# A Fourier mixing layer and a gated feed-forward layer in one kernel: where GpSimd's fold operations and the odd tables stand in the order of work

## The chip, the cores and the metric

The kernel runs on one core of a Trainium2 chip, in fp32. Its time is the device time of one execution in microseconds; smaller is better. The profile is of one execution, taken by the hardware profiler. The engines are called as in the profile: PE is TensorE's matmul and PEld its weight load, DVE is VectorE, ACT is ScalarE, POOL is GpSimd, SP issues most DMAs.

## The reference

Two layers follow one another.

- Mixing: X = FFT along the sequence, then FFT along the features, of x with shape (8, 3008, 256); only the real part is kept.
- Feed-forward, on the 8 x 3008 = 24064 rows of that result: gate = sigmoid(x @ w_gate), val = x @ w_val, out = (gate * val) @ w_out, with w_gate and w_val of 256 x 1536 and w_out of 1536 x 256.

```python
X = np.fft.fft(x, axis=1)
X = np.fft.fft(X, axis=2)
x = X.real.astype(np.float32).reshape(B * S, D)
gate = 1.0 / (1.0 + np.exp(-(x @ w_gate)))
val = x @ w_val
return (gate * val @ w_out).astype(np.float32)
```

## The kernel before

The real part of the two-dimensional transform needs only cosine and sine sums over the sequence, of folded data. For each batch the rows s, S-s, M+s and M-s (M = 1504) lie in four slots of one SBUF tile `x4`, 128 partitions x 4 slots x 6 rows x 256 features. **Folding** (`fold_ops`, L371) replaces the slots by their sums and differences, over the sequence and over the features. For batches 1 to 7 it is 24 operations, all on GpSimd, in this order: three `point` (L378) and a `first` (L382) for slots 0 and 1; the same four for slots 2 and 3 (operations 0 to 7); six `across` (L391; 8 to 13); three `feat` (a memset, L386, L388) on one pair of slots (14 to 16); four sums over halves of the rows (L407; 17 to 20); three `feat` on the other pair (21 to 23). After `feat` 14 to 16, six `turn` operations on VectorE (L418) rotate the odd half with the tangents in `ST[3]` and `ST[4]`.

The **sequence transform** of a batch (`whole`, `half`) is a run of matmuls of the folded tile with cosine and sine tables, in four groups of 24; it writes `ev` and `od`, which ScalarE and VectorE turn into `pk` and `qk` (`then`, `places`). The first two groups, of odd k, read `ST[1]` and the pair folded by operations 14 to 16; the last two, of even k, read the pair folded by operations 21 to 23. 

The **tables** come in two shapes. Batch 0 uses the one loaded at the start. At step 42 `table_again` loads another shape by four DMAs into the same place. `table_odd` then makes `ST[1]`, the table for odd k, out of neighbouring columns: two sums (L211), two halvings (L213, on ScalarE), and six small copies and memsets of the end columns (L214 to L220); and the tangents, three small operations on VectorE (L221 to L223).

The **main loop** (L843) has 576 steps: 8 batches x 6 chunks of up to 252 columns x 12 blocks of 128 of the 1536 hidden features, so 72 steps a batch. Step i does this, in program order: TensorE multiplies `G1`, the weights joined with the feature transform, by `pk` (`front_a`); ScalarE takes the sigmoid of step i-1 (`gate_a`), copies step i (`part`, L598) and puts the seeds of step i+1 into PSUM (`seed`, L582); VectorE and ScalarE finish the products of step i-1 (`gate_b`); TensorE multiplies by the output weights (`back`) and `G2` by `qk` (`front_b`). Three steps make a group, whose 9 products h are extended by 13 sums on GpSimd (L640, `H_SUMS`): seven when its second step is finished, six, some of them in the place of earlier ones, when its third is. `back`, for a group five steps earlier, reads only h in its part 0; blocks 13, 11 and 12 of sf in part 1; and five more blocks of sf in part 2. VectorE adds up the output of a finished chunk, two or three operations a step (`later`, L687), and transposes it.

What stands beside the main loop is put into a dictionary `side` by `at(i, f)`, and is emitted at the end of step i, after `front_b` and the `later` operations. Every engine runs its own instructions in the order in which they are emitted. So a fold operation stands in GpSimd's queue behind the sums of the steps before, and before those of the steps after it, and GpSimd reaches it some two steps later than TensorE passes the step that emits it.

Around the change: `folds(slots)` spreads 24 operations evenly over a list of steps `slots`. The sequence transform of batch b+1 is emitted at step `g0`: 64 for batch 1, and 72 b + 40 for the others, so 112 for batch 2 and 184 for batch 3. Before the change a slot is any step with i % 12 < 4, up to `g0`: 24 to 27, 36 to 39, 48 to 51 and 60 to 63 for batch 1; 72 to 75, 84 to 87, 96 to 99 and 108 to 111 for batch 2; and six such clusters for each later batch. Four successive slots get 6 operations for batches 1 and 2, and 4 for the others. `e_sums` at step 40 makes the rows `ed` with feature 128 of all later batches; `table_odd` stands at step 46.

Of the kernel before, what the change touches and what calls it, by code (L numbers as in the profile page):

```python
# [11 lines left out]
ALU = mybir.AluOpType  # L12
# [42 lines left out]
HP = 64  # L55
# [26 lines left out]
def kernel(  # L82
# [10 lines left out]
    nc = tc.nc  # L93
# [7 lines left out]
    NO = (M // 2) // 2  # L101
# [9 lines left out]
    NJ = NO // 2 + 1  # L111
# [17 lines left out]
    op = ctx.enter_context(tc.tile_pool(name="op", bufs=1))  # L129
# [3 lines left out]
    def mm(o, l, r, start, stop):  # L133
        nc.tensor.matmul(o, l, r, start=start, stop=stop, skip_group_check=True)  # L134

    def bank(name, other=None):
        if other is not None:
            return pso.tile([P, 512], F32, name=name, tag=f"po{other}")
        return psx.tile([P, 512], F32, name=name, tag="x")
# [4 lines left out]
    def load_x(b):  # L144
        X[b] = xp.tile([P, 4, NQ, D], F32, name="x4", tag="x4")
        for h in range(0, 4, 2):
            if b:
                nc.sync.dma_start(out=X[b][:, h : h + 2], in_=XR[b][:, h : h + 2])
            else:
                nc.sync.dma_start(out=X[b][0:NP, h : h + 2], in_=xf[b, :, h : h + 2])  # L150
# [3 lines left out]
    def mirror_x(b):  # L154


        copy = nc.sync.dma_start
        src = xf[b]
        dst = XR[b] = dram.tile([P, 4, NQ, D], F32, name=f"xr{b}")
        ops = [lambda: copy(out=dst[HP - 2 : HP, :, NQ - 1],  # L160
                            in_=zero[:, :, 0:D].to_broadcast([2, 4, D]))]

        def rows(par):
            copy(out=dst[par * HP : (par + 1) * HP, :, 0:N3], in_=src[0:HP, :, par:NQ:2])

        def mirror(par, q):
            t = M // 2 - 2 * q - par
            lo, p0, n = par * HP, t // NQ, HP - 2 * ((par, q) == (0, N3 - 1))
            copy(out=dst[lo : lo + n, :, N3 + q].rearrange("p h d -> h p d"),
                 in_=src[p0 - n + 1 : p0 + 1, :, t % NQ].rearrange("p h d -> h p d")[:, ::-1])  # L170
        for par in range(2):
            ops.append(lambda par=par: rows(par))
            ops += [lambda par=par, q=q: mirror(par, q) for q in range(N3)]
        return ops
# [3 lines left out]
    ST = [const.tile([P, 2, NQ, NE + NO], F32, name="st", tag="st")]  # L178
# [28 lines left out]
    def table_odd():  # L207

        odd, j4 = ST[0][:, :, :, NE:], ST[1]
        for t in range(2):  # L210
            nc.gpsimd.tensor_tensor(j4[:, t, :, 1 : NJ - 1], odd[:, t, :, 2::2], odd[:, t, :, 1 : NO - 1 : 2],  # L211
                                    op=ALU.add)
            nc.scalar.mul(j4[:, t, :, 1 : NJ - 1], j4[:, t, :, 1 : NJ - 1], 0.5)  # L213
        nc.gpsimd.tensor_copy(j4[:, 0, :, 0:1], odd[:, 0, :, 0:1])  # L214
        nc.gpsimd.memset(j4[:, 1, :, 0:1], 0.0)

        for par in range(2):
            rows = slice(par * HP, (par + 1) * HP)
            nc.gpsimd.tensor_copy(j4[rows, par, :, NJ - 1 :], odd[rows, par, :, NO - 1 :])
            nc.gpsimd.memset(j4[rows, 1 - par, :, NJ - 1 :], 0.0)  # L220
        nc.vector.reciprocal(ST[4], odd[:, 0, :, 0])  # L221
        nc.vector.tensor_tensor(ST[3], odd[:, 1, :, 0], ST[4], op=ALU.mult)
        nc.vector.tensor_scalar(out=ST[4], in0=ST[3], scalar1=-1.0, scalar2=None, op0=ALU.mult)  # L223

# [227 lines left out]
    def half(b, w, d, blk, sn, other=None):  # L454


        c0, n = ((0, NE), (NE, 2 * NJ if b else NO))[blk]
        ev, od = [bank(name, other and other[i])[:, 0:n] for i, name in enumerate(("ev", "od"))]

        def sums(*qs):  # L460
            for q in sorted(qs, key=lambda q: q % 2):
                mm((ev, od)[q % 2], w(q), ST[0][0:NP, int(sn), q, c0 : c0 + n], q < 2, q >= NQ - 2)

        def both():

            for r in range(2):
                for q in range(N3):
                    for par, sum_ in enumerate((ev, od)):
                        rows = slice(par * HP, par * HP + HP - 1 - (par and q == N3 - 1))
                        if blk:  # L470
                            out_, wq = sum_[:, r * NJ : (r + 1) * NJ], q + N3 * r
                            tab = ST[1][rows, r ^ int(sn), q]
                        else:
                            out_, wq = sum_[:, r::2], q + N3 * (r ^ int(sn))
                            tab = ST[0][rows, int(sn), q, r:NE:2]
                        mm(out_, w(wq)[rows], tab, q == 0 and r == 0, q == N3 - 1)

        def then():
            a = evp.tile([P, 2 * NJ], F32, name="a", tag="a")
            if b and blk:  # L480
                for par, sum_ in enumerate((ev, od)):
                    f = a[:, par * NJ : (par + 1) * NJ]
                    nc.scalar.copy(f, sum_[:, 0:NJ])
                    for r, op_ in enumerate((ALU.add, ALU.subtract)):
                        nc.vector.tensor_tensor(ST[2][:, par, r::2], f[:, r : NJ - 1 + r],  # L485
                                                sum_[:, NJ + r : 2 * NJ - 1 + r], op=op_)
                return lambda: places(d, blk, sn, ST[2][:, 0], ST[2][:, 1])
            a = a[:, 0:n]
            nc.scalar.copy(a, ev)
            return lambda: places(d, blk, sn, a, od)  # L490
        return sums, then, both

    def places(d, blk, sn, ev, od):
        nc.vector.tensor_tensor(d[:, blk : blk + 2 * ev.shape[1] - 1 : 2], ev, od, op=ALU.add)
        lo, hi = (od, ev) if sn else (ev, od)
        top = M - blk
        nc.vector.tensor_tensor(d[:, top : top - 2 * NO + 1 : -2], lo[:, 0:NO], hi[:, 0:NO],  # L497
                                op=ALU.subtract)

    def whole(b, blk, what):  # L500
        _, then, both = seq_group(b, blk, what, (2, 3) if what else (0, 1))
        both()
        return then()

    def seq_start(b):
        PQE[b] = [pqp.tile([P, NK + 1], F32, name=name, tag=name) for name in ("pk", "qk")]
        if not b:
            PQE[b].append(op.tile([P, NK + 1], F32, name="ek", tag="os"))
        for t in PQE[b]:
            nc.vector.memset(t[:, NK:], 0.0)  # L510
# [279 lines left out]
    def at(i, *fs):  # L790
        side.setdefault(i, []).extend(fs)
# [14 lines left out]
    i0 = NFT  # L806
# [7 lines left out]
    at(3 * i0, e_fold)  # L814
    at(3 * i0 + 4, lambda: e_sums()())
    at(3 * i0 + 6, table_again)
    at(3 * i0 + 10, table_odd)
    for i in range(i0, count, i0):
        at(i - 8, lambda i=i: e_rows(i))

    for b in range(B - 1):
        s0 = b * per
        g0 = s0 + 3 * i0 + 4 if b else 5 * i0 + 4


        slots = [i for i in range(s0 - 2 * i0 if b > 1 else s0 if b else 2 * i0, g0) if i % i0 < 4]

        def folds(slots, b=b):
            ops = fold_ops(b + 1, 2)
            for i, f in enumerate(ops):  # L830
                at(slots[i * len(slots) // len(ops)], f)
            for i, f in enumerate(TURN.pop(b + 1)):
                at(slots[-4 + i * 4 // 6], f)
        at(slots[0] - 1, lambda slots=slots, folds=folds: folds(slots))
        at(g0 - 2, lambda b=b: seq_start(b + 1))
        for blk in (1, 0):
            at(g0, *[lambda b=b, blk=blk, what=what: whole(b + 1, blk, what)() for what in range(2)])
        if b < B - 2:
            at(g0 + 1, lambda b=b: load_x(b + 2))
            for i, f in zip(calm(s0 if b else 3 * i0), mirror_x(b + 2)):  # L840
                at(i, f)
# [80 lines left out]
```

## Time and profile before

| | us |
|---|---|
| median of 3 runs | 1974.49 |
| lowest and highest run | 1964.23, 1974.6 |
| the profiled execution | 1966.45 |
| its span, first to last instruction | 1964.6 |
| PE busy | 1920.6 |
| POOL busy | 1639.9 |
| DVE busy | 1567.0 |
| ACT busy | 1341.0 |

A row of a group of instructions gives the line, the engine, the operation, what it writes and reads, the shape, how often it runs, its busy time in all, the mean ns of one, and the idle time of the engine before it with what ended it. A row in order of time gives start, length, engine, line, operation and tiles, and in brackets the engine's idle time before it and what ended that. A row of a stretch gives its ends and length, then the busy time of each engine with its number of instructions, the granted TensorE clock as a share of full speed, and the DMA share and rate. All matmuls have line L134, that of a helper; they are told apart by their tiles: `pf<-pk,G` is `front_a`, `pf<-qk,G` is `front_b`, `po` is `back`, `ev` and `od` are the sequence transform.

### The profile page before, as it was taken

How to read it: one execution, taken by the hardware profiler on the slowest of the kernel's cores; microseconds unless marked ns; L12 is line 12 of the kernel's file. 1: busy time of each engine (PE TensorE's matmuls, PEld its weight loads, DVE VectorE, ACT ScalarE, POOL GpSimd, SP SyncE). 2: the span in 40 equal slices, each digit the busy share in tenths (PEclk: the TensorE clock that was granted, in tenths of full speed). 3: DMA queues.
4: the chain of work that ended last, by engine and by line, in shares of the span. 5: the costliest groups of instructions: out<-in, count | busy, mean ns of one | idle time of the engine just before them, and what ended most of it. 6: DMA issues, size and time to landing. Idle time of an engine off the chain costs nothing.

```text
span 1964.6 us, 34539 instructions
## 1 busy us (share of the span) xinstructions
PE 1920.6 (98%) x11252; PEld 1791.5 (91%) x11252; DVE 1567.0 (80%) x3271; ACT 1341.0 (68%) x3124; POOL 1639.9 (83%) x2851
## 2 busy tenths in 40 slices
PE   6999899999999999999999999999999999999997
PEld 4889789998999999999999999999999999999997
DVE  7888797887788877888778887788878887777777
ACT  3567657665777767776777767777677776777775
POOL 3779898997889978897889878998788896777776
PEclk8999999999999999999999999999999999999999
DMA  8361413112012120222113121211210110011011
GB/s 269 89 133 27 102 39 110 46 24 78 18 46 52 21 78 14 54 51 64 29 22 77 21 78 22 44 53 20 81 20 14 19 23 14 14 21 21 14 19 27
DMA packets 169746, 96.78 MB, mean 49 GB/s; under 512 B 133858, under 2 KB 161636, under 8 KB 167020
## 3 DMA queue, kind: packets, MB, share of 16 engines
q1 hardware_dynamic: 167596, 94.02, 20.0%
q8 instruction: 90, 1.47, 0.3%
q10 hardware_dynamic: 1940, 0.56, 0.2%
q14 instruction: 88, 0.72, 0.1%
q0 software_dynamic: 32, 0.00, 0.0%
HBM read 69.83 MB, written 46.71 MB: 59 GB/s over the span
## 4 chain that ended last, share of the span: by engine, by line
PE 90%; DVE 5%; POOL 3%; ACT 1%; DMA 1%; issue 0%; SPq 0%; DVEq 0%; ACTq 0%; POOLq 0%
PE pf L134 47%; PE po L134 39%; PE ev L134 2%; POOL sf L640 2%; DVE c L687 1%; PE od L134 1%; DMA x<-in_xf_dram 1%; DVE h L636 1%; PE ps L134 1%; DVE z L622 1%; ACT z L635 0%; DVE st L485 0%; POOL x L407 0%; DVE pk L497 0%; POOL x L388 0%
## 5 line engine op out<-in xcount | busy, mean ns | idle before, releaser
L640 POOL TENSOR_TENSOR sf<-h 128x168 f32<-128x168 f32 (+1 forms) x960 | 552.3, 593 | 199.8 <-DVE h L636 199.7
L640 POOL TENSOR_TENSOR sf<-h,sf 128x168 f32<-128x168 f32 (+1 forms) x1152 | 661.5, 593 | 60.1 <-DVE h L636 60.1
L134 PE MATMUL pf<-qk,G 128*128 128x252 f32 (+1 forms) x2304 | 583.2, 376 | 7.8 <-ACT ae L598 5.6
L134 PE MATMUL pf<-pk,G 128*128 128x252 f32 (+1 forms) x2304 | 584.3, 376 | 0.0
L636 DVE TENSOR_TENSOR h<-z 128x252 f32<-128x252 f32 (+1 forms) x576 | 300.3, 521 | 332.1 <-ACT z L635 331.7
L582 ACT ACTIVATE pf<-ek,ge 128x252 f32<-128x252 f32 (+1 forms) x1128 | 531.5, 471 | 18.5
L134 PE MATMUL po<-sf,wf 128*128 128x168 f32 (+1 forms) x3072 | 530.8, 306 | 0.0
L598 ACT ACTIVATE ae<-pf 128x504 f32<-128x504 f32 (+1 forms) x569 | 335.0, 589 | 238.9 <-PE pf L134 238.4
L687 DVE TENSOR_TENSOR c<-c 128x168 f32<-128x168 f32 (+1 forms) x949 | 485.4, 542 | 5.5 <-ACT c L664 0.3
L134 PEld LDWEIGHTS pf<-pk,G 128*128 128x128 f32 x2304 | 437.0, 190 | 53.2 <-issue 2.3
L134 PEld LDWEIGHTS po<-sf,wf 128*128 128x128 f32 x3072 | 473.6, 190 | 8.3
L134 PE MATMUL po<-h,wf 128*128 128x168 f32 (+1 forms) x2688 | 477.1, 306 | 0.1
L134 PEld LDWEIGHTS po<-h,wf 128*128 128x128 f32 x2688 | 428.9, 191 | 17.1 <-DVE wf L357 0.3
L134 PEld LDWEIGHTS pf<-qk,G 128*128 128x128 f32 x2304 | 409.9, 190 | 35.3 <-ACT ae L598 7.4
L622 DVE TENSOR_TENSOR z<-ae,pf 128x504 f32<-128x504 f32 (+1 forms) x569 | 377.6, 664 | 21.3 <-ACT h L617 20.7
L617 ACT ACTIVATE h<-pf 128x252 f32<-128x252 f32 (+1 forms) x576 | 217.9, 378 | 161.2 <-PE pf L134 151.5
L635 ACT ACTIVATE z<-z 128x252 f32<-128x252 f32 (+1 forms) x576 | 231.6, 402 | 95.5 <-DVE z L622 74.2
L634 DVE TENSOR_TENSOR h<-h,pf 128x252 f32<-128x252 f32 (+1 forms) x576 | 231.9, 403 | 0.0
L640 POOL TENSOR_TENSOR sf<-sf 128x168 f32<-128x168 f32 (+1 forms) x192 | 111.6, 581 | 15.0
L640 POOL TENSOR_TENSOR sf<-sf,h 128x168 f32<-128x168 f32 (+1 forms) x192 | 107.4, 559 | 0.0
L134 PE MATMUL ev<-st,x 63*128 63x189 f32 (+3 forms) x372 | 77.1, 355 | 14.1 <-DVE x L388 7.5
L134 PEld LDWEIGHTS ev<-st,x 63*128 63x128 f32 (+1 forms) x372 | 63.5, 193 | 24.5 <-DVE x L388 7.9
(138 smaller groups left out, 905.4 us busy)
## 6 DMA issues: line engine op xcount, KB each, us to landing
x<-xr SPq DMA_DIRECT2D x14, 1536.0 KB
out_dram<-os SPq DMA_DIRECT2D x380, 56.0 KB
xr<-in_xf_dram SPq DMA_DIRECT2D x14, 768.0 KB
xr<-in_xf_dram SPq DMA_DIRECT2D x35, 256.0 KB
ek<-ed SPq DMA_DIRECT2D x39, 126.0 KB
out_dram<-os SPq DMA_DIRECT2D x288, 7.0 KB
st<-in_stab_dram SPq DMA_DIRECT2D x4, 1111.9 KB
x<-in_xf_dram SPq DMA_DIRECT2D x2, 1512.0 KB
```

The source lines that it names most:

```text
L134: nc.tensor.matmul(o, l, r, start=start, stop=stop, skip_group_check=True)
L582: nc.scalar.activation(PF[i][:, g], EK[i // NFT], AF.Copy, scale=ge[:, g, f : f + 1])
L598: nc.scalar.activation(AP[i], PF[i], AF.Copy, scale=2.0)
L617: nc.scalar.activation(H[p][:, fh, 0:n], PF[i][:, 0], AF.Sigmoid)
L622: nc.vector.tensor_tensor(z[:, :, ::-1], AP.pop(i), PF[i], op=ALU.subtract)
L634: nc.vector.tensor_tensor(h[:, fh, 0:n], h[:, fh, 0:n], PF.pop(i)[:, 1], op=ALU.mult)
L635: nc.scalar.activation(z[:, 0], z[:, 0], AF.Sigmoid)
L636: nc.vector.tensor_tensor(h[:, fh, n:], z[:, 0], z[:, 1], op=ALU.mult)
L640: nc.gpsimd.tensor_tensor(block(p, dst), block(p, a), block(p, b), op=(ALU.subtract, ALU.add)[op])
L687: engine.tensor_tensor(t[:, dst * R : (dst + 1) * R], *v, op=(ALU.subtract, ALU.add)[op])
```

## The change

`table_odd` no longer emits its work at once. It returns six functions, which are put at six successive steps, 54 to 59 (`at(4 * i0 + 6 + i, f)`; i0 is 12): the sum for the cosines, its halving, the sum for the sines, its halving, the ends, the tangents. The halvings are `tensor_scalar` on GpSimd in place of `mul` on ScalarE. The tangents stay on VectorE.

The slots of the folds end two steps sooner for every batch (`g0 - 2`), and for batches 1 and 2 a slot is any step with i % 12 < 6. So batch 1 has the slots 24 to 29, 36 to 41, 48 to 53, 60 and 61; batch 2 has 72 to 77, 84 to 89, 96 to 101, 108 and 109; 20 in place of 16, with 24 operations as before. Later batches have 22 in place of 24. The turns stay in the steps where they were: the last slot less one is now what the fourth slot from the end was.

```diff
     def table_odd():
         odd, j4 = ST[0][:, :, :, NE:], ST[1]
-        for t in range(2):
-            nc.gpsimd.tensor_tensor(j4[:, t, :, 1 : NJ - 1], odd[:, t, :, 2::2], odd[:, t, :, 1 : NO - 1 : 2],
-                                    op=ALU.add)
-            nc.scalar.mul(j4[:, t, :, 1 : NJ - 1], j4[:, t, :, 1 : NJ - 1], 0.5)
-        nc.gpsimd.tensor_copy(j4[:, 0, :, 0:1], odd[:, 0, :, 0:1])
...
-        nc.vector.reciprocal(ST[4], odd[:, 0, :, 0])
...
+        pool = nc.gpsimd
+
+        def inner(t):
+            pool.tensor_tensor(j4[:, t, :, 1 : NJ - 1], odd[:, t, :, 2::2], odd[:, t, :, 1 : NO - 1 : 2],
+                               op=ALU.add)
+
+        def half(t):
+            pool.tensor_scalar(out=j4[:, t, :, 1 : NJ - 1], in0=j4[:, t, :, 1 : NJ - 1], scalar1=0.5,
+                               scalar2=None, op0=ALU.mult)
+
+        def ends():
+            pool.tensor_copy(j4[:, 0, :, 0:1], odd[:, 0, :, 0:1])
+            pool.memset(j4[:, 1, :, 0:1], 0.0)
...
+        def tangent():
+            nc.vector.reciprocal(ST[4], odd[:, 0, :, 0])
...
+        return [lambda: inner(0), lambda: half(0), lambda: inner(1), lambda: half(1), ends, tangent]
...
-    at(3 * i0 + 10, table_odd)
+    at(4 * i0 + 5, lambda: [at(4 * i0 + 6 + i, f) for i, f in enumerate(table_odd())])
...
-        slots = [i for i in range(s0 - 2 * i0 if b > 1 else s0 if b else 2 * i0, g0) if i % i0 < 4]
+        slots = [i for i in range(s0 - 2 * i0 if b > 1 else s0 if b else 2 * i0, g0 - 2)
+                 if i % i0 < (4 if b > 1 else 6)]
...
             for i, f in enumerate(TURN.pop(b + 1)):
-                at(slots[-4 + i * 4 // 6], f)
+                at(slots[-1] - 1 + i * 4 // 6, f)
```

More of the change, by code (lines that the diff above doesn't have):

```diff
@@ L209, in table_odd @@
         odd, j4 = ST[0][:, :, :, NE:], ST[1]
-        for t in range(2):
-            nc.gpsimd.tensor_tensor(j4[:, t, :, 1 : NJ - 1], odd[:, t, :, 2::2], odd[:, t, :, 1 : NO - 1 : 2],
-                                    op=ALU.add)
-            nc.scalar.mul(j4[:, t, :, 1 : NJ - 1], j4[:, t, :, 1 : NJ - 1], 0.5)
-        nc.gpsimd.tensor_copy(j4[:, 0, :, 0:1], odd[:, 0, :, 0:1])
[L215 to L220, printed above, removed]
-        nc.vector.reciprocal(ST[4], odd[:, 0, :, 0])
-        nc.vector.tensor_tensor(ST[3], odd[:, 1, :, 0], ST[4], op=ALU.mult)
-        nc.vector.tensor_scalar(out=ST[4], in0=ST[3], scalar1=-1.0, scalar2=None, op0=ALU.mult)
+        pool = nc.gpsimd
[8 more added lines that the diff above has]
+            pool.memset(j4[:, 1, :, 0:1], 0.0)
+            for par in range(2):
+                rows = slice(par * HP, (par + 1) * HP)
+                pool.tensor_copy(j4[rows, par, :, NJ - 1 :], odd[rows, par, :, NO - 1 :])
+                pool.memset(j4[rows, 1 - par, :, NJ - 1 :], 0.0)
+        def tangent():
+            nc.vector.reciprocal(ST[4], odd[:, 0, :, 0])
+            nc.vector.tensor_tensor(ST[3], odd[:, 1, :, 0], ST[4], op=ALU.mult)
+            nc.vector.tensor_scalar(out=ST[4], in0=ST[3], scalar1=-1.0, scalar2=None, op0=ALU.mult)
+        return [lambda: inner(0), lambda: half(0), lambda: inner(1), lambda: half(1), ends, tangent]
     assert NPR == 6
```

## The prediction

> **What bounds the kernel now.** I read the page's busy shares, the chain of waits, the busy times by stretch, and each engine's instructions in order of time around every stretch where TensorE stood still. From the page:
>
> ```profile
> PE 1920.6 (98%) x11252; PEld 1791.5 (91%) x11252; DVE 1567.0 (80%) x3271; ACT 1341.0 (68%) x3124; POOL 1639.9 (83%) x2851
> ```
>
> TensorE is busy 98%, and beyond the first 125 us nearly all its idle time lies in a few places. A step is the time between the starts of two successive G x pk groups in TensorE's timeline: 3.12 us for chunks of 252 columns. Stretches cut at such starts (columns: time, length, busy us of PE, PEld, DVE, ACT, POOL, granted clock, DMA):
>
> ```profile
> 222.97:228.53 5.56, 3.40 (x20) 2.85 (x18) 4.26 (x8) 3.07 (x7) 4.62 (x12) 1.00 0.00 1
> 228.53:233.35 4.82, 4.82 (x19) 4.53 (x19) 3.14 (x9) 2.34 (x6) 3.63 (x7) 0.65 0.26 40
> 280.25:294.80 14.55, 11.88 (x116) 10.67 (x115) 12.49 (x26) 4.88 (x13) 12.58 (x23) 1.00 0.06 11
> 435.12:438.71 3.59, 3.39 (x19) 2.85 (x18) 3.44 (x8) 2.00 (x5) 3.51 (x6) 1.00 0.03 5
> 438.71:442.52 3.81, 3.42 (x20) 2.88 (x19) 3.66 (x8) 2.48 (x6) 3.81 (x6) 1.00 0.44 70
> 442.52:458.70 16.18, 13.51 (x115) 12.26 (x114) 12.55 (x26) 4.91 (x13) 12.64 (x23) 0.89 0.03 9
> 679.80:692.19 12.39, 12.12 (x115) 10.85 (x113) 11.00 (x23) 4.75 (x14) 9.51 (x18) 1.00 0.07 12
> ```
>
> These are steps 47, 48, 64, 110, 111, 112 and 184. Steps 64, 112 and 184 hold the sequence transform of batches 1, 2 and 3; 184 shows it undisturbed. In the chain of waits (total, times, longest) and in time order:
>
> ```profile
> ACT st L213 <- POOL st L211: 2.7, 2, 2.2
> PE ev L134 <- POOL x L388: 5.2, 2, 2.6
> ```
>
> ```profile
> 224.94 0.67 ACT L213 ACTIVATE st<-st 128x561 f32<-128x561 f32 x1 [2.24 <-POOL st L211]
> 227.57 1.12 PE L134 MATMUL pf<-qk,G 128*128 128x252 f32 x4 [2.16 <-ACT ae L598]
> 291.89 0.43 PE L134 MATMUL ev<-st,x 63*128 63x188 f32 x1 [2.61 <-POOL x L388]
> ```
>
> At step 47 ScalarE, in order, stands before the table's halving until GpSimd reaches the sum of L211; sigmoid, ae copy and seeds are behind it, and TensorE waits for ae. At steps 64 and 112 TensorE waits for the last fold (L388), which GpSimd finishes too late.
>
> GpSimd is the tight engine in folds. It owes 13 sums per three steps (L640), some 7.55 us when back to back (251.54 to 259.10), so it can work off about 1.8 us of anything else per three steps. Prices of the rest, from the groups of GpSimd in 320 to 455 us:
>
> ```profile
> L391 POOL TENSOR_TENSOR x<-x 128x512 f32<-128x512 f32 x6 | 8.2, 1384 | 0.1
> L378 POOL TENSOR_TENSOR x<-x 128x510 f32<-128x510 f32 x6 | 7.9, 1326 | 0.0
> L386 POOL TENSOR_TENSOR x<-x 128x254 f32<-128x254 f32 x6 | 4.6, 769 | 0.0
> L388 POOL TENSOR_TENSOR x<-x 128x254 f32<-128x254 f32 x6 | 4.6, 759 | 0.5
> L407 POOL TENSOR_TENSOR x<-x 128x384 f32<-128x384 f32 x4 | 4.3, 1088 | 0.0
> ```
>
> How late it may be: the second sum that L640 makes in a triple's last three-step group (block 12) is read as the last block product of TensorE's part 1. Unhurried it is there 6.5 us early; in batch 2's third cluster it is just in time:
>
> ```profile
> 410.65 1.89 POOL L640 TENSOR_TENSOR sf<-h,sf 128x168 f32<-128x168 f32 x3
> ```
>
> ```profile
> 411.73 0.83 PE L134 MATMUL po<-sf,wf 128*128 128x168 f32 x4
> ```
>
> Of these three, two take until about 411.9; the po group's second half, which reads block 12, starts at 412.0.
>
> **What the Trainium skill says.** "TensorE: Matmul & The Clock Gate", Part 1: the gate watches free-running windows of 3413 ns, and after an idle one halves the clock. The trace agrees: clock 0.65 over the 4.82 us of step 48 is 1.7 us lost, half of 3.4; after the 2.61 us at 289 no such loss follows. "GPSIMD Engine Reference", section 8: GpSimd shares its SBUF interfaces with VectorE, against instructions with two SBUF inputs. The trace agrees: three L687 sums take 1.85 us at 262.66, beside a full GpSimd, and 1.15 at 220.00. Same page, sections 3.1 and 4.1: one-input work near line rate, 1.03 cycles an element. No GpSimd tensor_scalar is in this trace.
>
> **The change, part by part.**
>
> *ScalarE's two halvings go (step 46).* With them the wait, and the five table operations of GpSimd at 223.69 to 226.75. Steps 47 and 48 become ordinary: 5.55 + 4.83 - 2 x 3.12 = **4.13 us** gained, the half-clock window included.
>
> *Batch 1's folds end at step 61, not 63.* Step 64 falls from 14.55 to about 12.3 (184's, less 0.05 for 246 columns), step 63 from 3.26 to 3.09: **2.42 us**.
>
> *Batch 2's end at 109, not 111.* Steps 110 to 112: 3.59 + 3.81 + 16.19 - 2 x 3.12 - 12.39 = **4.95 us**, of which 1.16 (110 and 111) is not GpSimd's: there TensorE waits for ae behind a late VectorE, and this need not go.
>
> Together 11.5 us.
>
> *What the wider clusters cost GpSimd.* The 24 fold operations of a batch take 8 x 1.3 (points, firsts), 6 x 1.33, 6 x 1.57 and 4 x 1.05, some 30 us. By clusters, now 6.7, 6.9, 8.4, 8.1; then 7.9, 9.6, 8.9, 3.3. Between clusters four triples lend 4 x 1.8 = 7.2, so the second cluster leaves a debt it did not leave. Added up by hand from 319.70, where GpSimd of batch 2 has just idled: block 12 of steps 87 to 89 is ready at 383.3, wanted at 383.8; the debt is 1.2 us when the third cluster begins (397.2 against 395.94); the third cluster then puts block 12 of steps 99 to 101 at 422.4 where it is wanted at 421.5. **0.94 us lost**, at step 105, with an error of +-0.7, as 64 us of work precede it. VectorE catches up in that pause, so I keep only 1.16 - 0.94 = **0.22 us** of its lateness at 110 and 111.
>
> For batch 1 the long pause for the ed row (2.87 us at 203.5, steps 40 and 41 take 11.8 us) clears the debt, and nothing is late before step 48. Then, on a clock 4.13 us earlier: fold operations 15 to 21 in steps 48 to 53, the table in 54 to 58, folds 22 and 23 in 60 and 61. Block 12 of steps 51 to 53 is ready at 255.0, wanted at 256.2; that of 54 to 56 at 265.0 + h, wanted at 265.6, with h for one halving; that of 57 to 59 at 273.3 + 2h, wanted at 274.8 and what was lost before.
>
> *h.* Bounds: below, 561 elements at 1.03 cycles of 1.2 GHz, 0.48 us, an estimate by the page; above, the two-input sum of the same size, 1.21 us (L211). Of two-input sums, 168 elements take 0.595 and 561 take 1.207, so 0.33 us is fixed; 0.33 + 0.48 = 0.8 us, which I take. Then **0.23 us lost** at step 57 (0 to 0.64), none at 60. The last fold is done at about 275.7 + 1.6 + 3.2 = 280.5; TensorE asks for it some 8.5 us after step 64 starts at 276: covered by 4 us.
>
> *Tangents moved to step 59 (VectorE).* Three operations of 0.16, 0.87 and 0.17 us (225.02 to 226.29). At 225 they lay in the stall. At step 59 VectorE is busy 2.97 of 3.12 us and behind it stand z and h of L622 to L636, then the turns of steps 60 to 63 (1.44 us for two). h is ready 7.3 us after its step's start at 59 and 8.3 at 61; at steps 109 and 110, where it reached 9.3, TensorE lost 1.16 us, while 8.7 at 108 cost nothing. Adding 0.4 to 1.2 for the tangents and 0.5 for a GpSimd that no longer rests at 60, the peak is 9.2 to 10: **1.2 us lost** at 61 to 63 (0.5 to 2.5).
>
> *The rest.* No DMA is moved: SP's queue holds the same issues at the same steps, and the table's loads, issued at 201, have long landed. The turns keep their steps; they and the last folds ran past one another unwaited before. Batches 3 to 7: two doubled slots, under 1.6 us each, against 5 us of earliness there: nothing, and up to 0.5 us each if that is gone.
>
> Sum: 11.50 - 0.94 - 0.22 - 0.23 - 1.2 = **8.9 us less**. The profiled execution took 1966.45 us (span 1964.6): 1957.6. The runs shown lie at 1964.23, 1974.49 and 1974.6, so that execution is 8 us under their median; from the median it is **1965.6**.
>
> **Rivals.** (1) No new wait: GpSimd's and VectorE's lateness stay under what TensorE needs: 11.5 us, 1963.0. For it: my errors are as large as the stalls. Against it: block 12 at 410.65 already had no margin. (2) VectorE and GpSimd become the bound of steps 50 to 63 and 84 to 111: both busy without rest for 50 us and slowing each other, losses of some 8 us, among them a half-clock window; about 3 us gained, 1971.5. For it: L687 at 1.85 against 1.15 us. Against: 101 to 109 were already so, and cost 0.11. (3) Slower: GpSimd's multiply is slow. Place: steps 55 and 57; each halving is paid by TensorE at steps 57 and 60, (h - 0.57) + (h - 0.93), and over 2 us a wait brings a half-clock window (1.7 us each). The other losses leave 9.1 us to eat: it decides from h = 3.6 us, three times the two-input sum; at 6 us it ends at 1979. Nothing but the absence of that operation in the trace speaks for it.
>
> **How the numbers follow.** Forecast 0.55, (1) 0.17, (2) 0.20, (3) 0.08. About 0.5%, 9.9 us, is what a measurement of this kernel can tell from no change: below 1964.6 or above 1984.4. The forecast lies 1 us on this side of the bound, and the runs' own spread of 10 us decides it: 0.45 faster, 0.55 same; (1) 0.75 and 0.25; (2) 0.25, 0.65 and 0.10; (3) half same, half slower. Faster 0.43, same 0.50, slower 0.07. Range: from 1954, the forecast on the level of the profiled execution with (1)'s gain, to 1972, which takes in (2).
>
> **What would show it.** Right: no wait for L211; steps 47 and 48 at 3.12; steps 64 and 112 at 12.3 to 12.6 with no wait for L388; two fewer half-clock windows; TensorE waiting for sf about step 105, and for ae at 61 to 63; the new multiply at 0.8 us. Wrong: that multiply over 2 us, waits for sf at steps 89 or 57 above 1 us, a half-clock window near 250 to 280 or 420, or step 64 still above 13.5.

## The result, and the profile after

| us | before | after |
|---|---|---|
| median of 5 runs each | 1974.49 | 1959.49 |
| lowest and highest | 1964.23, 1976.15 | 1955.37, 1963.5 |
| the profiled execution | 1966.45 | 1959.49 |
| its span | 1964.6 | 1957.5 |
| from step 16's start to the last step's | 1822.96 | 1813.81 |

The ratio of after to before is 0.994, with a 95% interval of 0.9918 to 0.9962: the whole interval lies below 1, but it reaches across 0.995, the 0.5% that the prediction names as the least that can be told from no change. The last row needs a word, because all experiments are read by it. A kernel's runs spread over 8 to 12 us, and much of that arises before step 16: in the profiled executions of all the kernels below that start-up took 118 to 126 us (120.53 in before, 122.74 in after). Two profiled executions of after, of 1959.49 and 1955.77 us, differ by 3.6 us in the start-up and by 0.12 from step 16 on (1813.81 and 1813.69), with no step more than 0.03 us different. So the change is worth **9.15 us in the main loop**; the profiled execution shows 7.0, as its start-up took 2.2 us longer, and the medians show 15.0, as the runs of before happened to lie high (in three later series its median was 1970.66, 1971.37 and 1968.96). Not all of the 9.15 is sure to come: a stretch at half the clock, a *half-clock window* of 3.41 us, cost before 1.7 us each at steps 48 and 112, and costs after 1.7 us at steps 41 and 42. Whether a wait meets such a window is partly chance, as the experiments show.

From the page of after, the engines' busy time; lines of the changed kernel are those of before plus 10 (L640 is L650, L687 is L697, L388 is L398, L391 is L401, L407 is L417, L598 is L608, L622 is L632):

```profile
PE 1915.8 (98%) x11252; PEld 1788.6 (91%) x11252; DVE 1600.5 (82%) x3271; ACT 1334.1 (68%) x3122; POOL 1645.6 (84%) x2853
```

VectorE runs the same 3271 instructions in 33.5 us more: the sums into c (L697) take 512.4 us in place of 485.4 and the products h (L646) 316.5 in place of 300.3, while some others are shorter. The stretches of steps 47, 48, 64, 91, 112 and 184 of after (columns as before):

```profile
227.80:230.93 3.13, 3.13 (x20) 2.95 (x19) 2.70 (x6) 2.15 (x5) 1.86 (x4) 1.00 0.00 0
230.93:234.05 3.12, 3.12 (x19) 2.94 (x18) 2.23 (x7) 2.15 (x5) 2.72 (x5) 1.00 0.26 40
282.10:294.29 12.19, 12.04 (x115) 10.88 (x113) 11.11 (x23) 4.77 (x14) 11.88 (x22) 1.00 0.06 13
374.97:379.48 4.51, 3.39 (x19) 2.85 (x18) 4.36 (x8) 2.00 (x5) 4.51 (x8) 1.00 0.19 67
...
444.00:456.02 12.02, 12.02 (x115) 11.10 (x114) 11.15 (x25) 5.06 (x14) 7.52 (x15) 1.00 0.08 17
677.12:688.66 11.54, 11.54 (x115) 10.84 (x113) 10.11 (x23) 4.53 (x13) 6.52 (x13) 1.00 0.06 10
```

Steps 47 and 48 are ordinary, at full clock. Steps 64 and 112 no longer wait for the last fold. Step 184, which had served as the undisturbed measure, has itself become shorter. Step 91, ordinary before, takes 4.51 us, and TensorE (PE) is busy for 3.39 of them. Set side by side, step by step (us; steps not listed agree within 0.11):

| steps | before | after | difference |
|---|---|---|---|
| 47, 48 | 5.55, 4.83 | 3.12, 3.12 | -4.13 |
| 64 | 14.55 | 12.19 | -2.36 |
| 112 | 16.19 | 12.02 | -4.17 |
| 110, 111 | 3.59, 3.81 | 3.42, 3.32 | -0.66 |
| 184, 256, 328, 400, 472 | 12.39 each | 11.54 each | -4.25 |
| 41, 42 | 6.37, 3.15 | 7.30, 4.83 | +2.62 |
| 58, 60, 63 | 3.12, 3.08, 3.26 | 3.44, 3.25, 3.87 | +1.09 |
| 91, 103, 105 | 3.12 each | 4.51, 3.95, 3.58 | +2.67 |

What ended TensorE's waits, from the waits of after in two stretches. In 225 to 283 us, steps 47 to 63:

```profile
PEld po L134 <- POOL sf L650: 0.9, 3, 0.4
```

and in 368 to 442 us, steps 89 to 111:

```profile
ACT z L645 <- DVE z L632: 21.6, 19, 3.0
...
PEld pf L134 <- ACT ae L608: 2.9, 4, 1.4
```

In batch 1 GpSimd's block sums are late; in batch 2 they never are. There ScalarE's copy ae is late, because ScalarE stands before VectorE's z. Around step 91, in order of time:

```profile
371.92 4.00 POOL L401 TENSOR_TENSOR x<-x 128x512 f32<-128x512 f32 x3
...
373.39 3.30 DVE L697 TENSOR_TENSOR c<-c 128x168 f32<-128x168 f32 x3
...
377.31 0.41 ACT L645 ACTIVATE z<-z 128x252 f32<-128x252 f32 x1 [2.96 <-DVE z L632]
...
378.53 1.12 PE L134 MATMUL pf<-qk,G 128*128 128x252 f32 x4 [1.12 <-ACT ae L608]
```

Three sums of 168 elements on VectorE take 3.30 us beside three fold operations of 512 elements on GpSimd. One by one, two of the sums meet a fold and last 1.39 and 1.28 us, the third meets a block sum and lasts 0.67; the product h before them met the first fold and lasted 1.47. Then z, the sigmoid's queue, ae and TensorE follow late in turn. And in the row sums at step 41:

```profile
205.06 4.32 POOL L401 TENSOR_TENSOR x<-x 128x512 f32<-128x512 f32 x3
...
206.66 1.60 DVE L507 TENSOR_TENSOR er<-a 7x376 f32<-7x376 f32 x1
...
209.52 1.12 PE L134 MATMUL pf<-qk,G 128*128 128x252 f32 x4 [3.81 <-ACT ae L608]
...
210.47 1.79 PE L134 MATMUL pf<-pk,G 128*128 128x252 f32 x4
```

L507 took 0.87 us there in before, and TensorE's gap was 2.87, not 3.81; what follows at 210.47 is at half clock.

### The profile page after: what moved, and what is told of

Its sections match the earlier page's. It is cut to its first block, busy times and chain, and to the rows that moved or that the text cites. A ratio compares the mean times of both kernels' runs of the same rounds, so it can differ in the third digit from the quotient of the medians.

```text
span 1957.5 us, 34550 instructions
## 1 busy us (share of the span) xinstructions
PE 1915.8 (98%) x11252; PEld 1788.6 (91%) x11252; DVE 1600.5 (82%) x3271; ACT 1334.1 (68%) x3122; POOL 1645.6 (84%) x2853
## 3 DMA queue, kind: packets, MB, share of 16 engines
q8 instruction: 90, 1.47, 0.3%
## 4 chain that ended last, share of the span: by engine, by line
PE 90%; POOL 4%; DVE 3%; DMA 2%; ACT 1%; issue 0%; ACTq 0%; DVEq 0%; SPq 0%; POOLq 0%
PE pf L134 47%; PE po L134 39%; PE ev L134 2%; POOL sf L650 2%; DVE c L697 1%; DMA st<-in_stab_dram 1%; PE od L134 1%; PE ps L134 1%; DMA ge<-G 1%; DVE h L646 1%; DVE z L632 0%; ACT z L645 0%; POOL x L401 0%; DMA raw<-in_moe_w_gate_dram 0%; POOL x L417 0%
## 5 line engine op out<-in xcount | busy, mean ns | idle before, releaser
L650 POOL TENSOR_TENSOR sf<-h 128x168 f32<-128x168 f32 (+1 forms) x960 | 551.0, 593 | 196.9 <-DVE h L646 196.8
L650 POOL TENSOR_TENSOR sf<-h,sf 128x168 f32<-128x168 f32 (+1 forms) x1152 | 663.4, 595 | 46.7 <-DVE h L646 46.7
L646 DVE TENSOR_TENSOR h<-z 128x252 f32<-128x252 f32 (+1 forms) x576 | 316.5, 549 | 296.8 <-ACT z L645 294.9
L697 DVE TENSOR_TENSOR c<-c 128x168 f32<-128x168 f32 (+1 forms) x949 | 512.4, 571 | 5.5 <-ACT c L674 0.3
L608 ACT ACTIVATE ae<-pf 128x504 f32<-128x504 f32 (+1 forms) x569 | 335.3, 589 | 216.1 <-PE pf L134 214.7
L632 DVE TENSOR_TENSOR z<-ae,pf 128x504 f32<-128x504 f32 (+1 forms) x569 | 377.7, 664 | 15.6 <-ACT h L627 15.2
L650 POOL TENSOR_TENSOR sf<-sf 128x168 f32<-128x168 f32 (+1 forms) x192 | 111.5, 581 | 15.1
L650 POOL TENSOR_TENSOR sf<-sf,h 128x168 f32<-128x168 f32 (+1 forms) x192 | 109.3, 569 | 0.0
L134 PE MATMUL ev<-st,x 63*128 63x189 f32 (+3 forms) x372 | 73.3, 347 | 11.5 <-DVE x L398 9.0
L674 ACT COPY c<-po 128x504 f32<-128x504 f32 (+1 forms) x144 | 80.2, 557 | 3.1 <-PE po L134 3.1
```

The costliest lines, as they stand in the source:

```text
L608: nc.scalar.activation(AP[i], PF[i], AF.Copy, scale=2.0)
L632: nc.vector.tensor_tensor(z[:, :, ::-1], AP.pop(i), PF[i], op=ALU.subtract)
L646: nc.vector.tensor_tensor(h[:, fh, n:], z[:, 0], z[:, 1], op=ALU.mult)
L650: nc.gpsimd.tensor_tensor(block(p, dst), block(p, a), block(p, b), op=(ALU.subtract, ALU.add)[op])
L674: (nc.vector.tensor_copy if t == 1 or t == 3 and not last else nc.scalar.copy)(C[0][:, 3 * t * R : 3 * (t + 1) * R], PO[t][:, 0 : 3 * R])
L697: engine.tensor_tensor(t[:, dst * R : (dst + 1) * R], *v, op=(ALU.subtract, ALU.add)[op])
```

## The experiments

In the expectations V is the theory that VectorE is held up by GpSimd's fold operations, and P that GpSimd itself comes late with its block sums. The loop is the time from step 16 to the last step: 1822.96 before, 1813.81 after.

### The table's part alone

After, with the folds' slots and turns as before:

```diff
+        slots = [i for i in range(s0 - 2 * i0 if b > 1 else s0 if b else 2 * i0, g0) if i % i0 < 4]
...
+                at(slots[-4 + i * 4 // 6], f)
```

> Only the table part of the change; the folds are as before. The wait for L211 at steps 47 and 48 goes (4.13 us gained). Both theories: GpSimd now carries 7 us of table work (its multiply took 1.62 us in the changed kernel) into the last cluster of folds, so by the sums of GpSimd's own work the last fold of batch 1 is done near 294 us where TensorE wants it near 286: step 64 grows from 14.55 to some 20 to 23 us, and the two parts of the change are not additive. The main loop from step 16 on ends 2 to 6 us later than before. If instead the folds of batch 1 are not what GpSimd's table work delays, step 64 stays at 14.6 and the loop is 4 us shorter.

Measured: 1969.58 us, before beside it 1970.66; loop 1826.27, **3.3 us slower than before**. Steps 47 and 48 give back the same 4.13, but step 64 grows from 14.55 to 21.31. From the timeline of this run:

```profile
286.60 0.58 PE L134 MATMUL ev<-st,x 63*128 63x189 f32 x1 [2.78 <-POOL x L398]
...
293.18 0.68 PE L134 MATMUL ev<-st,x 63*128 63x188 f32 x1 [2.94 <-POOL x L398]
```

The table's work of steps 54 to 59 stands in GpSimd's queue ahead of the last folds, at 60 to 63, and makes them late; between the two rows lie matmuls of 0.52 us that take 0.32 in after, at half clock. The two parts of the change are not additive: the table at steps 54 to 59 needs the folds to end sooner.

### The folds' part alone

Before, with the new slots and turns; the table stays at step 46, with ScalarE's halvings.

```diff
+        slots = [i for i in range(s0 - 2 * i0 if b > 1 else s0 if b else 2 * i0, g0 - 2)
+                 if i % i0 < (4 if b > 1 else 6)]
...
+                at(slots[-1] - 1 + i * 4 // 6, f)
```

> Only the fold part; the table is made at step 46 with ScalarE's halvings as before. The stall at steps 47 and 48 stays (2.4 us, or 4.1 with a half-clock window). Losses of the changed kernel at steps 58, 60 and 63 (0.32, 0.17 and 0.60 us) go, if GpSimd's table work made them; if VectorE beside the folds made them alone they stay. Steps 91, 103 and 105 (1.39, 0.83, 0.45 us lost) and the five gains of 0.85 us at the transforms of batches 3 to 7 are as in the changed kernel. Main loop from step 16 on: 5 to 7 us shorter than before.

Measured: 1959.14 us; loop 1815.52, 7.44 less than before. Steps 64 and 112 at 11.88 and 12.01, 184 and its like at 11.54, 91, 103 and 105 longer by 1.29, 0.78 and 0.43, 41 and 42 by 0.92 and 1.68. So all of these belong to the folds. The losses at 58, 60 and 63 are gone or small (3.15, 3.10, 3.33), so they need the table's work on GpSimd; but 55 and 62 are longer by 0.44 and 0.35. Of the table's part, the wait stays, with 47 at 5.53; yet 48 is at 3.15, not 4.83:

```profile
229.89 1.12 PE L134 MATMUL pf<-qk,G 128*128 128x252 f32 x4 [2.13 <-ACT ae L598]
```

The wait of 2.16 us at this place met a half-clock window in before, the same wait of 2.13 met none here. So 1.7 of the 7.44 us are not the folds', and 1.7 of the 4.13 gained at 47 and 48 are a loss that need not have come. Alone, the parts make +3.3 and -7.4; together -9.15.

### Four slots in twelve, all ending two steps sooner

```diff
-                 if i % i0 < (4 if b > 1 else 6)]
+                 if i % i0 < 4]
```

> The changed kernel with four slots of twelve for every batch, still ending two steps sooner (14 slots for batches 1 and 2). Theory V (folds in the fifth and sixth step of twelve lie beside the output sums of VectorE, which begin there, and slow them, and TensorE waits for VectorE): the losses at steps 91, 103 and 105 (2.67 us in all) go, and those at 41 and 42 (0.94 us and a half-clock window of 1.7) too. Theory P (GpSimd is late with sf because the folds of batch 2 add up): clusters of 8 to 9 us on seven operations leave block 12 of steps 96 to 101 only 0.3 to 0.5 us early, so TensorE's losses near 102 to 105 stay at about 1 us. V: 3 to 5 us shorter than the changed kernel from step 16 on. P: the same within 1 us.

Measured: median 1956.49 of 7, ratio to before 0.9931 (0.9908 to 0.9954); loop 1813.34, within 0.5 of after's. Without the wider clusters the loss at 91 falls from 1.39 to 0.35 and those at 103 and 105 go, but small ones stand at 79, 83, 107 and 112 (0.9 in all) and at 110 and 111 (0.3), and 41 and 42 are 0.5 longer. The 3 to 5 us that V expected did not come; the total is what P expected, but not its place, as 103 and 105 are at 3.12 and 3.15. Beside the table's move, the sooner end brings the whole gain of the folds; six slots in place of four are worth nothing.

### Batches 3 to 7 ending as before

```diff
+        slots = [i for i in range(s0 - 2 * i0 if b > 1 else s0 if b else 2 * i0, g0 if b > 1 else g0 - 2)
...
+                at(slots[-1] - (3 if b > 1 else 1) + i * 4 // 6, f)
```

> The changed kernel, but the folds of batches 3 to 7 end where they ended before. If the earlier end is what shortened steps 184, 256, 328, 400 and 472 from 12.39 to 11.54 us, they are 12.39 again and the main loop is 4.2 us longer than in the changed kernel; VectorE's operations on pk (L504, L507) take 0.88 and 1.07 us beside the last fold in place of 0.55. If it came from anything else in the change, they stay at 11.54.

Measured: 1967.28 us with a start-up of 125.3; loop 1818.80, 5.0 above after. Steps 184 to 472 are back at 12.39 each (4.2 of the 5.0; most of the rest is a longer step 41). VectorE's busy time is back at 1565.8 us, so the 33.5 us more in after come from where the folds of batches 3 to 7 now lie; outside the five transforms TensorE loses nothing by them. Why these batches gain is seen in the timeline of before in step 184:

```profile
686.76 0.88 DVE L494 TENSOR_TENSOR pk<-st 128x376 f32<-128x376 f32 x1
687.32 0.91 POOL L388 TENSOR_TENSOR x<-x 128x254 f32<-128x254 f32 x1
687.57 1.07 DVE L497 TENSOR_TENSOR pk<-st 128x376 f32<-128x376 f32 x1
...
689.50 0.57 PE L134 MATMUL ev<-st,x 63*128 63x189 f32 x2 [0.27 <-DVE st L485]
```

and after:

```profile
684.09 0.55 DVE L504 TENSOR_TENSOR pk<-st 128x376 f32<-128x376 f32 x1
...
684.56 0.54 DVE L507 TENSOR_TENSOR pk<-st 128x376 f32<-128x376 f32 x1
```

The last folds ran on GpSimd while VectorE made pk out of the transform's sums; two steps sooner, they no longer do. The two operations are together 0.86 us shorter, and the step 0.85. TensorE waited for no fold there, but for VectorE behind one.

### No folds of batch 1 in steps 39 to 41

```diff
+                 if i % i0 < (4 if b > 1 else 6) and (b or i not in (39, 40, 41))]
```

> The changed kernel with no fold of batch 1 in steps 39 to 41, so that GpSimd has no fold operation beside the four operations that write er on VectorE. Theory V (a two-input operation of VectorE is held while GpSimd runs a fold): the last er operation (L507) falls from 1.60 to 0.9 us or less, step 41 from 7.30 to 6.4 or less, and with the shorter gap the half-clock window behind it (1.7 us at step 42) may go as well. If the longer gap at 41 came from elsewhere (when the sums of x8 were ready, say), step 41 stays at 7.3. The larger clusters at 24 to 29 and 48 to 53 that this makes may cost up to 1 us at 58 to 63.

Measured: 1959.45 us; loop 1816.66. The row sum is at 0.87 us again and TensorE's gap at 2.91, so the 0.94 of step 41 comes from the folds beside it. But the gap still met a half-clock window (41 and 42: 7.22 and 4.00), where before's gap of 2.87 had met none. With three slots fewer, the clusters at 24 to 29 and 48 to 53 hold nine fold operations each, in place of eight and seven; steps 31 to 35 are 1.2 longer, 57 is 1.29 and 60 is 1.86 longer.

### The halvings on ScalarE, at steps 59 and 60

```diff
-            pool.tensor_scalar(out=j4[:, t, :, 1 : NJ - 1], in0=j4[:, t, :, 1 : NJ - 1], scalar1=0.5,
-                               scalar2=None, op0=ALU.mult)
+            nc.scalar.mul(j4[:, t, :, 1 : NJ - 1], j4[:, t, :, 1 : NJ - 1], 0.5)
...
+    at(4 * i0 + 5, lambda: [at(4 * i0 + i, f) for i, f in zip((6, 11, 8, 12, 10, 11), table_odd())])
```

> The changed kernel with the two halvings on ScalarE, at steps 59 and 60, five and four steps behind the sums of 54 and 56, so that ScalarE need not wait for GpSimd. GpSimd has 3.2 us less to do. The prediction's account (GpSimd late with sf at steps 60 and 63 because of the table work, and the multiply was 1.62 us and not 0.8): the losses at 60 and 63 (0.17 and 0.60 us) go, the one at 58 (0.32 us, where TensorE waits for ae) stays. If VectorE's tangents make the losses at 60 and 63, they stay. No wait for L213 on ScalarE above 0.5 us.

Measured: 1964.37 us with a start-up of 126.3; loop 1815.13, 1.3 above after. A miss in its main point. The multiply takes 0.65 us on ScalarE, and the block sums are in time (block 12 of the two groups 2.0 and 4.4 us early in place of 0.05), but the waits of 255 to 300 us show the next in line, ae, some 0.3 us late in most steps:

```profile
ACT z L644 <- DVE z L631: 12.1, 11, 1.7
...
PEld pf L134 <- ACT ae L607: 2.3, 7, 0.6
```

Steps 59 to 62 and 64 grow by 0.2 to 0.6 each, and 63 is 0.4 shorter. ScalarE stands before a late VectorE, and has 1.3 us of halvings more to do at 59 and 60; which of the two makes ae late was not separated.

### Batch 2's across operations replaced by memsets

GpSimd stays as busy (1536 elements written per memset), but reads nothing; the results of batch 2 are left uncomputed.

```diff
         def across(e, blk, q):
+            if b == 2:
+                e.memset(x4[:, 1 - blk], 0.0)
+                return
```

> The changed kernel, but each of the six across operations of batch 2 (steps 84 to 88) is a memset of 1536 elements in place of a two-input sum of 512, so batch 2's result is left uncomputed. GpSimd is busy about as long (1.3 to 1.5 us each, by the memsets of 40 and 252 elements), but reads nothing. Theory V (two-input sums of VectorE are held by GpSimd's reads and not by its being late): the loss of 1.39 us at step 91 goes, and three L697 sums there take some 1 us and not 3.3. Theory P (GpSimd is late): step 91 stays at 4.4 us. A memset that also holds VectorE would leave 91 as it is, with the sums at 3 us.

Measured: 1955.43 us; loop 1812.59. Step 91 is at 3.12. From the timeline of this run:

```profile
369.04 4.25 POOL L402 MEMSET x<- 128x1536 f32 x3
...
369.30 0.93 DVE L700 TENSOR_TENSOR c<-c 128x168 f32<-128x168 f32 x3
```

GpSimd is taken for 4.25 us and VectorE's three sums last 0.93 us, not 3.30. P would have them late all the same. Step 103 is at 3.12 too, although three L417 operations lie there as in after; VectorE was earlier and its sums had partly run ahead of them. That this follows from step 91 is only argued. Step 105 stays long.

### Across and row halves in pieces of half the size, batches 1 and 2

```diff
+            for p in [slice(r, r + 1) for r in range(q.start, q.stop)] if b in (1, 2) else [q]:
+                e.tensor_tensor(x4[:, 1 - blk, p], x4[:, 0, p], x4[:, 2, p],
...
```

The four sums over halves of rows are cut likewise.

> After, with the six across operations and the four sums over halves of rows of batches 1 and 2 each made in two operations of half the size (256 and 192 elements); the same work, ten operations more a batch. Theory V in a sharper form: in the trace of after, a sum of VectorE into c lasts 0.32 us alone, 1.34 when it meets an across operation (L401, 1.33 us), 1.12 when it meets L417 (1.07 us), 0.66 when it meets a block sum of L650 (0.59 us): it is held until the one operation of GpSimd that it meets is done. Then it should last 0.8 to 0.9 beside the halves (0.3 fixed and half the rest); the loss at step 91 falls from 1.39 to 0.2 to 0.7, that at 103 from 0.83 to below 0.5, and the row operation at step 41 from 1.60 to about 1.1, so that step 41 is 0.3 to 0.5 shorter. If VectorE is slowed in proportion to what GpSimd reads, whatever its pieces: 91 and 103 as in after, within 0.2. GpSimd pays some 0.25 us for each added operation, 2.5 a batch: if its lateness were what counts (theory P), 91 and 103 would be longer than in after, and steps 60 and 63 too.

Measured: 1955.58 us; loop 1813.36. **Steps 91, 103, 58, 110 and 111 are all at 3.12**, and step 41 is 0.66 shorter than in after. From its timeline:

```profile
203.20 1.06 DVE L509 TENSOR_TENSOR er<-a 7x376 f32<-7x376 f32 x1
...
368.72 4.79 POOL L402 TENSOR_TENSOR x<-x 128x256 f32<-128x256 f32 x6
368.96 2.40 DVE L699 TENSOR_TENSOR c<-c 128x168 f32<-128x168 f32 x3
...
379.85 1.15 PE L134 MATMUL po<-sf,wf 128*128 128x168 f32 x4 [0.27 <-POOL sf L652]
```

The same elements in twice as many operations take GpSimd 4.79 us in place of 4.00 and hold a sum of VectorE 0.8 us in place of 1.1. But now GpSimd is late, as the last row shows: 60, 93, 105 and 112 are longer than in after by 0.94, 0.82, 1.11 and 0.73. Both limits are real; which one is met depends on how the same work is cut.

### The tangents at step 49

```diff
+    at(4 * i0, lambda: [at(4 * i0 + i, f) for i, f in zip((6, 7, 8, 9, 10, 1), table_odd())])
```

> The changed kernel with the three tangent operations on VectorE at step 49, where VectorE is not full, in place of step 59. The prediction's account of the tangents (0.4 to 1.2 us of VectorE ahead of z and h, which TensorE waits for at 61 to 63) has the losses at 60 to 63 (0.77 us) fall to 0.3 or less. If GpSimd's lateness with sf makes them (its two halvings of 1.62 us), steps 60 and 63 stay at 3.25 and 3.87 us.

Measured: 1955.06 us; loop 1813.94 (after 1813.81). Step 60 is unchanged and 63 is 0.28 longer. The tangents at step 59 cost nothing.

### Clusters of batches 1 and 2 two steps sooner, four slots in twelve

The table's sums at steps 51 and 52, its ends at 53, tangents at 49, halvings on ScalarE at 56 and 57.

```diff
+    at(4 * i0, lambda: [at(4 * i0 + i, f) for i, f in zip((3, 8, 4, 9, 5, 1), table_odd())])
...
-                 if i % i0 < (4 if b > 1 else 6)]
+                 if (i if b > 1 else i + 2) % i0 < 4]
```

> A version that should beat the changed kernel if theory V holds: batches 1 and 2 fold in the steps with (i + 2) % 12 < 4, two steps earlier than before in each cluster, so that GpSimd, which comes 2.5 steps later, is through when VectorE's output sums begin; the table's sums at 51 and 52, the ends at 53, the tangents at 49, the halvings on ScalarE at 56 and 57. Theory V: losses at 91, 103 and 105 go (2.67 us), at 60 and 63 too (0.77), and at 41 and 42 (2.6 us) if the folds are through before er: 4 to 6 us less than the changed kernel from step 16 on. Theory P: only the 0.77 us.

Measured: median 1955.82 of 4, ratio to before 0.9926 (0.9898 to 0.9953); loop 1810.81, **12.15 less than before and 3.0 less than after**. Steps 60, 63, 91, 103, 105, 110 and 111 are all at 3.08 to 3.12; what is left is 57, at 4.43, where TensorE waits 0.7 us for a block sum, and 41 and 42. The 4 to 6 us that V expected are missed by these, 41 and 42 by chance in part, as the next run shows. As the clusters, the table's steps and the halvings were changed together, the gain is not divided among them. By its steps it beats both kernels; in medians it can't be told from after, as both intervals overlap.

### The same with the table at steps 45 to 50

```diff
+    at(4 * i0 - 4, lambda: [at(4 * i0 + i, f) for i, f in zip((-3, 1, -2, 2, -1, 1), table_odd())])
```

> The shifted folds of the version before, with the table made in the gap that GpSimd has after step 42: sums at 45 and 46, ends at 47, halvings on ScalarE at 49 and 50, tangents at 49. If the 1.30 us that the shifted version loses at step 57 is GpSimd, late with sf behind the table's sums of 51 and 52, it goes, and steps 43 to 64 are all at their undisturbed length: 1.4 us less than the shifted version from step 16 on, 13.5 us less than before. If it is ScalarE's halvings at 56, it moves to step 50.

Measured: median 1960.16 of 6, ratio 0.9945 (0.9925 to 0.9965), loop 1812.45. A miss: 57 is mended, but the table now stands in front of the cluster, its block sums are late at 54, and a half-clock window follows (54 and 55: +3.57 and +0.49); 62 to 64 are longer by 2.0 in all. Up to step 45 this kernel and the one before it do the same, and yet steps 41 and 42 take 2.9 us less here. The gap is the same, first in the kernel with shifted clusters, then here:

```profile
203.88 2.04 PE L134 MATMUL pf<-qk,G 128*128 128x252 f32 x4 [2.98 <-ACT ae L607]
...
212.25 1.12 PE L134 MATMUL pf<-qk,G 128*128 128x252 f32 x4 [2.98 <-ACT ae L607]
```

There the matmuls after it take 2.04 us at half clock, here 1.12 at the full one.

### After, once more

> The changed kernel once more, beside the version above on one chip. From step 16 on as in its first profile, within the 1.7 us of a half-clock window at steps 41 and 42: 9.2 us less than before.

Measured beside the last: median 1958.43 of 6, before 1968.96 of 11, ratio 0.9946 (0.9925 to 0.9966); loop 1813.69. This is the repeat named at the start.

## Why the prediction was right, and where its working was not

The forecast was -8.9 us; the loop shows -9.15, and the median fell inside the range. From the median the forecast was 1965.6 us; the measured 1959.49 lies lower because the runs of before happened to lie high. The gains that it named came as it said, but its losses did not, and a gain of 4.25 us was missed. That the sum is right is luck: its errors cancel.

- *Halvings off ScalarE, 4.13.* Right to the hundredth for these two runs: the wait for L211 is gone, and so is the half-clock window at 229. But only 2.4 of it is the wait's own; the window of 1.7 was absent beside the same wait in the run with the folds' part alone.
- *Batch 1's folds sooner, 2.42.* Step 64 gave 2.36. Step 63 was put 0.17 shorter and is 0.60 longer.
- *Batch 2's folds sooner, 4.95.* Steps 110 to 112 gave 4.83. Of the 1.16 at 110 and 111, 0.50 was kept; the prediction kept 0.22. Step 112 fell to 12.02, below the 12.39 that stood for undisturbed, most likely for the reason that shortened 184.
- *Block 12 late at step 105, 0.94.* This step failed: block 12 of that group was 1.4 us early, and that of steps 87 to 89 1.8. The losses, 2.67, lie at 91, 103 and 105, where TensorE waits for ae behind a late VectorE. The prediction had the contention in view, as rival (2), and a long stretch of it: "101 to 109 were already so, and cost 0.11". What it missed is that the hold lasts as long as one GpSimd operation. The block sums that VectorE meets all the time are short (0.6 us); the L401 operations of the second cluster (1.3) and the L417 of the third (1.1) are long. Memsets and halved pieces show this for 91, and the halved pieces for 103; for 105 it rests on the trace alone.
- *h = 0.8 us, 0.23 lost at 57.* A term mis-sized: h measured 1.62 us (1613 and 1633 ns), above the upper bound of 1.21. The loss is at steps 60 and 63, 0.77, with 0.9 us of waits for sf; 57 was spared. There the prediction had named the right blocks and the wrong steps: blocks 12 of steps 54 to 56 and of 57 to 59 are read at 60 and 63, not at 57 and 60, and TensorE took both up 0.05 us after they were ready. Its sum with h at 1.62 would be 1.7. Rival (3) decides from 3.6 us and was not met; its "over 2 us a wait brings a half-clock window" is contradicted by the prediction's own 2.61 us at 289, which brought none.

```profile
L217 POOL TENSOR_SCALAR st<-st 128x561 f32<-128x561 f32 x2 | 3.2, 1623 | 0.1
...
L213 POOL TENSOR_TENSOR st<-st 128x561 f32<-128x561 f32 x2 | 2.4, 1209 | 0.0
```

These two rows, from GpSimd's groups in 230 to 300 us of after, say it: the operation with one input is slower than that with two. The lower bound had come from the Trainium skill, "GPSIMD Engine Reference", section 3.1, which has 1.03 cycles an element for the smallest loop bodies; the prediction took it for any operation with one input. No run here shows it for this one, and the measurement decides.

- *Tangents, 1.2.* This term falls: moved to step 49, they change nothing to the good. At steps 59 to 63 of after, h was ready 7.5 to 8.2 us after its step's start, not 9.2 to 10.
- *"The long pause for the ed row clears the debt, and nothing is late before step 48."* Wrong in its second half. The folds placed at the pause made a row sum longer (0.94), and the longer gap met a half-clock window (1.68): 2.62 us.
- *Batches 3 to 7, nothing.* Wrong, 4.25 us gained. The stretch of step 184 was taken as undisturbed because TensorE waited for no fold in it; its 0.27 us behind VectorE, and VectorE's operations of 0.88 and 1.07 us, were on the timeline. It was the largest miss, and it pays for the others.

Rival (1), 11.5 us, falls, and so does (2) as a size: the losses in its two stretches are 3.8 us and 0.5 kept, half of its 8, with no half-clock window there. Of the signs, one fewer half-clock window was seen, not two, as a new one came at step 41.

Slips that change nothing: the fold prices as printed add up to 32 us, not 30, as the two short `first` are counted as points; and the chances add up to 0.515 for the same and 0.06 for slower, not 0.50 and 0.07.

## What to carry to other kernels

When work is moved on GpSimd, ask not only when it is done but which two-input operations of VectorE run beside it, and for how long each single GpSimd operation lasts: cutting it shorter frees VectorE, at a price for GpSimd (here 0.26 us for each piece more). A stretch used as the clean measure of a stage must itself be looked at for stretched operations. And edits that are harmless together can be harmful alone: here the table's move without the sooner end costs 3.3 us.

## What the runs showed of the hardware

The sums into c on VectorE (two inputs in SBUF, 168 or 164 elements), sorted by the GpSimd operation under way when each begins, in the individual records of the trace of after, the memset from its own run; a few other operations, each met by six sums at most, are left out:

| GpSimd meanwhile | its mean us | sums | median us of a sum |
|---|---|---|---|
| none, or just ending | | 154 | 0.33 |
| L650, two inputs, 168 elements | 0.59 | 755 | 0.66 |
| L417, two inputs, 384 elements | 1.06 | 10 | 1.12 |
| L401, two inputs, 512 elements | 1.33 | 12 | 1.34 |
| L217, one input, 561 elements | 1.62 | 3 | 0.32 |
| memset, 1536 elements | 1.38 | 5 | 0.33 |

So beside operations of two inputs a sum is not slowed in proportion: it ends some 0.2 us after the end of the one GpSimd operation that it meets (the three of step 91 at 374.78, 376.10 and 376.69; GpSimd's operations at 374.59, 375.91 and 376.50). GpSimd is held as well: a block sum of 168 elements takes 0.54 us with no such operation of VectorE beside it, and 0.63 when a sum into c begins during it.

The row of L217 is not the whole of it. Nine of the traces have sums that begin during this multiply, 29 in all: the 23 that begin 0.80 us or more after its start last 0.32 to 0.33 us, but the six that begin in its first 0.34 us last 0.71 to 0.78 and end about halfway through it. So the multiply holds a sum in its first half; why was not tested.

The Trainium skill, "GPSIMD Engine Reference", section 8, has it that the interfaces are shared against VectorE's instructions with two SBUF inputs. The runs agree for GpSimd's operations of two inputs and for the first half of the multiply; the memsets, which read nothing, held none of the five sums that began 0.16 to 0.87 us into one.

On the clock, pairs of equal waits at the same place met a half-clock window or did not: 2.91 us (folds cleared) and 2.87 (before), 2.98 and 2.98 in the two kernels with shifted clusters, 2.16 (before) and 2.13 (the folds' part alone). One window costs 1.7 us. The Trainium skill, "TensorE: Matmul & The Clock Gate", Part 1, calls the windows free-running; these pairs agree, and a forecast can put the loss only as a chance. The page has the clock halved after an idle window of about 3.4 us; here waits of 2.16 and 2.91 us were enough, so the measurement decides.
